# A sign-flipped sine plane, full-row narrow matmuls, merged LayerNorm statistics, other banks, a moved radix-4 inverse and a DMA transpose in a fused S4 convolution and gated MLP

## Chip, cores, metric

One core of one Trainium2 chip. The metric is device microseconds (us) of one execution. Medians are over the fast runs of a kernel; the runs of one kernel here lie within about 1.2% of each other. A profile shows one execution; its span is about 1.8 us shorter than that execution's own time, which need not be the median: the profile of e7 below is of its slowest run, that of e8 of its fastest.

## The reference, cut to what matters

```python
def reference(u, A..., w_gate, w_up, w_down):          # u: 1 x 2048 x 640, bf16
    K = einsum("dn,dnl,dn->dl", C, exp(dt*A*l), dt*B).real   # 640 filters of 2048 taps, 128 modes each
    y = irfft(rfft(pad(layernorm(u))) * rfft(pad(K)))[:L] + layernorm(u) * Dskip
    h = u + y                                            # stage A: the long convolution
    g, v = layernorm(h) @ w_gate, layernorm(h) @ w_up    # stage B: 640 -> 1728
    return h + (sigmoid(g) * v) @ w_down                 # 1728 -> 640
```

Of the kernel before, what the change touches and what calls it, by code (L numbers as in the profile page):

```python
# [26 lines left out]
R4 = (2,)  # L27
AT = {"eb": -38.3, "ea0": -22.2, "tb0": -12.8, "cb": -5.3, "bb0": 10.0, "st0": -13.2, "ta0": 20.7, "ch0": -25.4, "A0": 1.0, "st1": -127.2,
      "st2": -38.2, "st3": 34.0, "tb1": 45.8, "bb1": 28.9, "n0": -8.7, "ta1": 48.0, "ch1": 54.1, "A1": -23.3, "tb2": 49.0, "bb2": 68.1,
      "ea1": 70.7, "n1": 53.4, "ta2": 71.2, "ch2": 33.5, "A2": 32.8, "tb3": 73.0, "bb3": 75.3, "n2": -7.5, "s0": 66.5, "l0": -14.7,  # L30
      "i0": 94.9, "ta3": -15.7, "ch3": -6.7, "A3": -12.7, "n3": 0.8, "s1": 76.0, "l1": -16.4, "i1": 219.0, "i2": -7.7, "LATER": 49.5,
      "LATER2": 98.7, "EARLY": -11.7, "s2": 58.8, "p0": -14.4, "p1": -3.4, "p2": -13.4, "PW": 1, "w0": 29.5, "w1": -19.5, "w2": 66.8,
      "w3": 82.8, "DT": (0, 0, 0, 0), "NG": (1, 0, 0, 0), "TAIL": -45.1, "NA": (1, 2, 0, 0), "SA": (2, 0, 0, 3),
      "K": (42.3, 65.1, 109.8, 202.7), "F": (-18.0, 64.3, 14.3, 46.5), "G": (2.6, 0.5, 2.3, 0)}
# [9 lines left out]
M_SHIFT = (0, 1, 2, 8, 9, 10)  # L44
B_STEPS = ((1, 2, (0, 1, 1), 2), (2, 4, (0, 2, 1), 1), (4, 8, (0, 4, 1), 0), (8, 12, (0, 4, 1), 3), (12, 16, None, 4),
           (16, 18, (0, 16, 8), 5), (18, 21, (12, 17, 2), 5))

# [6 lines left out]
def host_consts():  # L54
    k = np.arange(P)
    fs = np.stack([256 * np.arange(2)[:, None] + k, 511 - 256 * np.arange(2)[:, None] - k], axis=1)
    om = 2 * np.pi * (fs + 0.5) / 1024
    conj = np.array([1.0, -1.0])[:, None]

    G = np.zeros((P, 2, 2, 2, 4, P))  # L60
    n = 4 * np.arange(P)[:, None] + np.arange(4)
    ang = om[None, :, :, None, :] * n[:, None, None, :, None]
    G[:, :, :, 0] = np.cos(ang)
    G[:, :, :, 1] = -np.sin(ang) * conj[None, None, :, :, None]

    lag = np.arange(2048)
    tap = lag.astype(np.float32).astype(ml_dtypes.bfloat16).astype(np.int64)
    KM = np.zeros((P, 2, 2, 2, NK, P))
    for d in range(NB):
        S = np.zeros((2049, 2, 2, P), np.complex128)  # L70
        ls = lag[max(0, LB * d - LB + 1):LB * d + LB]
        np.add.at(S, tap[ls], np.exp(-1j * om[None] * (ls[:, None, None, None] - LB * d)))
        for q, j in enumerate(KD[d]):
            for m in range(4):
                blk = S[B_VAL[4 * j + m] + 8 * np.array(A_EXP)]
                KM[32 * m:32 * m + 32, :, :, 0, KI[d] + q] = blk.real
                KM[32 * m:32 * m + 32, :, :, 1, KI[d] + q] = blk.imag * conj

    IV = np.zeros((P, 4, 2, 2, P))
    nn = 4 * np.arange(P)[None, :] + np.arange(4)[:, None]  # L80
    a = om[:, 0].T[:, None, :, None] * nn[None, :, None, :]
    IV[:, :, :, 0] = np.cos(a) / LB
    IV[:, :, :, 1] = -np.sin(a) / LB
    IV = np.concatenate([IV.reshape(P, 16, P), -IV[:, 1::2].reshape(P, 8, P)], axis=1)

    sel = np.zeros((P, 2, 32))
    sel[32, 0, 31] = 1.0
    for (b, t), rows in SEL.items():
        if b:
            sel[list(rows), 1, FIRST[b] + t - ROWS[b][0]] = 1.0  # L90

    pick = np.zeros((P, 4, 32))
    for c in range(4):
        pick[4 * np.arange(32) + c, c, np.arange(32)] = 1.0
    last = np.zeros((P, 3, 4, NL))
    for c in range(4):
        last[c, 0, c, 0:4] = 1.0
        last[c, 1, c, 4:10] = 1.0
        last[c, 2, c, 10:14] = 1.0
    one = np.zeros((P, 32))  # L100
    one[64, 0] = 1.0
    mult = [4.0 * (31 - 2 * k) for k in range(16)] + [1.0, 2.0]
    dg = np.eye(P)[:, None] * (np.array(mult) * 2.0 ** -13)[None, :, None]
    return {"dg": dg.reshape(P, -1), "ident": np.eye(P), "G": G.reshape(P, -1), "KM": KM.reshape(P, -1), "IV": IV[:, :20].reshape(P, -1), "IVN": IV[:, 20:].reshape(P, -1), "sel": sel.reshape(P, -1),
            "pick": pick.reshape(P, -1), "last": last.reshape(P, -1), "one": one}
# [27 lines left out]
def full_kernel(tc, ins, out):  # L133
# [56 lines left out]
    pick = cload(cp, "pick", [P, 4, 32])  # L190
    last = cload(cp, "last", [P, 3, 4, NL])
# [3 lines left out]
    cor = cp.tile([P, 40], F32, name="cor")  # L195
    xc = cp.tile([P, 40], BF16, name="xc")
    edge = cp.tile([96, D], BF16, name="edge")
    sy.dma_start(edge[64:65, :], ins["A_Dskip"].rearrange("(o d) -> o d", o=1))
# [32 lines left out]
    mg = tabp.tile([P, 2, P], F16, name="mg")  # L231
    ones = tabp.tile([P, 1], F16, name="ones")
    nc.gpsimd.memset(ones[:], 1.0)
    nc.gpsimd.memset(mg[:, 0], MAGIC16 / P)
    nc.gpsimd.memset(mg[:, 1], 0.25 / P)

    def turns(items, o, w):
# [3 lines left out]
        for a in range(2):  # L241
            MM(ps[:, a, 0:m * w], lhsT=mg[:, 0], rhs=bc(ones[:], [P, m * w]), start=True, stop=False)
            for q in range(m):
                src, dk, oo = items[a * m + q]
                for i in range(2):
                    MM(ps[:, a, q * w:q * w + w], lhsT=dg[:, dk, :], rhs=fr[:, src, i, o + oo:o + oo + w], start=False, stop=(q == m - 1 and i == 1))  # L246
        v = ps[:, :, 0:m * w].bitcast(I16).rearrange("p a (n t) -> p a n t", t=2)[:, :, :, 0]

        def quarter():
            for a in range(2):  # L250
                MM(ps[:, a, 0:m * w], lhsT=mg[:, 1], rhs=bc(ones[:], [P, m * w]), start=False, stop=True, skip_group_check=True)
# [8 lines left out]
    st = cp.tile([P, 16, 2, 6], F32, name="ln_st", tag="ln_st")  # L260
# [33 lines left out]
    def trig_b(c):  # L294
        M = T["MB", c] = tabp.tile([P, 2, 6, W], BF16, name="tabMB", bufs=2)
        v, quarter = turns([(0, 16, 0), (0, 17, 0), (0, 15, 0), (1, 16, 0), (1, 17, 0), (1, 15, 0)], W * c, W)
        act_fn(TWO(M[:, 1]), v, AF.Sin, scale=SIN_SCALE16)
        quarter()
        act_fn(TWO(M[:, 0]), v, AF.Sin, scale=SIN_SCALE16)

    def bases_b(c):
        M = T["MB", c]
        for ri in range(2):
            V(M[:, ri], EB[:, :, W * c:W * c + W], M[:, ri], ALU.mult)

# [68 lines left out]
    def chain_b(c):  # L374
        X, M = T["B", c], T["MB", c]
        tS = tabp.tile([P, 8 * W], BF16, name="tS")
        for d0, d1, src, mi in B_STEPS:
# [3 lines left out]
            if src is None:  # L381
                for ri in range(2):
                    s4 = X[:, ri, 0:16, :].rearrange("p (a b) w -> p a b w", a=2)[:, :, 0:2, :]
                    t4, d4 = (v.rearrange("p (a b) w -> p a b w", a=2) for v in (t[:, ri], dst[:, ri]))
                    for o4, pl in ((t4, 1), (d4, 0)):
                        V(o4, s4, bc(M[:, pl:pl + 1, mi:mi + 1, :], [P, 2, 2, W]), ALU.mult)
            else:
                s = X[:, :, slice(*src), :]
                V(t, s, bc(M[:, 1:2, mi:mi + 1, :], [P, 2, n, W]), ALU.mult)
                V(dst, s, bc(M[:, 0:1, mi:mi + 1, :], [P, 2, n, W]), ALU.mult)  # L390
# [6 lines left out]
    def ln_stats(st, mv, src, r):  # L397
        for hh in range(2):
            nc.vector.bn_stats(st[:, r, hh, :], src(r)[:, 320 * hh:320 * hh + 320])  # L399
        nc.vector.bn_aggr(mv[:, r, :], st[:, r, :, :].rearrange("p a b -> p (a b)"))  # L400
# [53 lines left out]
    def kmm(c):  # L454
# [16 lines left out]
        def diagonal(g1, kts):  # L471
# [8 lines left out]
            MM(pv[0:32, 0], lhsT=one[64:65, :], rhs=edge[64:65, dc].rearrange("p (g c) -> p g c", c=4), start=False, stop=True, tile_position=(64, 0))  # L480
            for c4 in range(4):
                MM(pl[:, :, c4], lhsT=last[:, 2, c4, :], rhs=kts[:, :, 80 + c4], start=not c4, stop=False)
            nc.scalar.copy(kv[:, :, 4 * g1:4 * g1 + 4 * GC], ps[:, 0, 0:20 * GC].rearrange("p (j x) -> p j x", j=5))
            for q in range(2):
                MM(ps[0:NL, 1, 0:4 * GC], lhsT=last[0:1, q, 0, :], rhs=kv[0:1, 3 + q, 4 * g1:4 * g1 + 4 * GC], start=False, stop=(q == 1))
# [32 lines left out]
    def prod(c, fs):  # L518
# [7 lines left out]
        for ft in fs:  # L526
            V(t1[:, ft], Z0[:, ft, :, :, o:o + W], S01[:, 0, ft, :, :, o:o + W], ALU.mult)
            V(t2[:, ft], Z0[:, ft, :, :, o:o + W], S01[:, 0, ft, :, ::-1, o:o + W], ALU.mult)
# [10 lines left out]
    def inv0(c, fs=((0, 1),), done=None):  # L539
# [6 lines left out]
        for a in range(2):  # L546
            with tc.issue_after(T["mm"]):
                MM(pv[:, a], lhsT=ident[:], rhs=hv[:, a], start=True, stop=False)
            if a:
                MM(ps[96:128, a, W:2 * W], lhsT=sel[32:33, 0, :], rhs=edge[32:33, o:o + W], start=False, stop=False, tile_position=(32, 96))  # L550
# [102 lines left out]
    st2 = cp.tile([P, 4, 4, 6], F32, name="ln2_st", tag="ln_st")  # L653
# [47 lines left out]
    for r in range(4):  # L701
        for q in range(NC - 2):
            nc.vector.bn_stats(st2[:, r, q, :], h[:, r, W * q:W * q + W])
# [9 lines left out]
    for r in range(4):  # L713
        nc.vector.bn_stats(st2[:, r, NC - 2, :], h[:, r, W * (NC - 2):W * (NC - 1)])

    def done(pv):
        for r in range(4):
            nc.vector.bn_stats(st2[:, r, NC - 1, :], pv[:, r // 2, r % 2])
# [8 lines left out]
    def edges(psp):  # L727
# [6 lines left out]
        sy.dma_start(dcor[:], ct[0:8, :])  # L734
        for b, (t0, t1) in ROWS.items():
            sy.dma_start(xc[16 * FIRST[b]:16 * (FIRST[b] + t1 - t0), :], lanes(x2d[512 * b + 508 + t0:512 * b + 508 + t1, :]))
        sy.dma_start(cor[:], lanes(dcor[:]))
        V(xc[:], xc[:], cor[:], ALU.add)
        sy.dma_start(lanes(dxc[:]), xc[:])
# [88 lines left out]
def mlp(tc, sc, xp, yp, cp, hs, st, mv, rstd, nmr, gu, Wd, ident, oh, ln_coef, ln_stats_act, later, edges, products, inverse, load_h, patch):  # L828
# [23 lines left out]
    def turn(b):  # L852
# [6 lines left out]
        if b and AT["PW"]:  # L859
# [7 lines left out]
        for dc in range(5):  # L867
            pt = psg_p.tile([P, 4, 128], BF16, name="ml_pt", tag="ml_pg")
# [16 lines left out]
    pso.append(pso_p)  # L885
# [5 lines left out]
    for b in range(NB):  # L891
# [29 lines left out]
        for lp in (0, 2):  # L921
            if lp and AT["PW"]:
# [22 lines left out]
            for k in range(2):  # L945
# [3 lines left out]
                for c in range(2):  # L949
                    if b < NB - 1:  # L950
                        tb = Wd[:, 15, 320 * c:320 * c + 320]
# [69 lines left out]
```

## The kernel before: the parts the change touches

The kernel builds tables of complex powers, makes the filter taps from them on TensorE, transforms taps and rows into a block spectrum by matmuls with constant matrices, multiplies the spectra on VectorE, and transforms back. Row block 0 (512 of the 2048 rows) is finished first. Then four MLP blocks run, and the spectral products and inverse transforms of the next row block are woven into each of them. All instructions are traced in one order and then reordered by a scheduler that obeys a table of tuned priorities, `AT`; each engine executes its own list in that order.

```python
R4 = (2,)                       # row block whose inverse uses the radix-4 shortcut (half the matmuls)
AT = {...tuned priorities..., "PW": 1, "DT": (0, 0, 0, 0), "NA": (1, 2, 0, 0), "SA": (2, 0, 0, 3), ...}
# PW: which PSUM banks; DT: DMA transpose per row block; NA / SA: rows normalized / measured by ScalarE

def chain_b(c):                 # powers from powers: complex products, plane 0 cosine, plane 1 sine
    for d0, d1, src, mi in B_STEPS:
        ...
        V(t,   s, sine of step mi,   ALU.mult)
        V(dst, s, cosine of step mi, ALU.mult)
        V(dst[:, 0], dst[:, 0], t[:, 1], ALU.subtract)
        V(dst[:, 1], dst[:, 1], t[:, 0], ALU.add)

def diagonal(g1, kts):          # taps from diagonals, on TensorE, 32-column tiles
    ... 16 matmuls of pick ...
    MM(pv[0:32, 0], lhsT=one[64:65, :], rhs=edge[64:65, dc]..., tile_position=(64, 0))     # one row
    ...
    for q in range(2):
        MM(ps[0:NL, 1, ...], lhsT=last[0:1, q, 0, :], rhs=kv[0:1, 3 + q, ...], ...)        # one row

def turn(b):                    # normalized rows of the next MLP block, transposed for TensorE
    if AT["DT"][b]:
        for i in range(4):
            nc.sync.dma_start(lnT[:, :, i, :], ln2[:, i, :], transpose=True)
        return
    if b and AT["PW"]:          # into the banks of the output accumulators
        ...
    for dc in range(5):         # into the gate banks, one bank per channel chunk
        ...

# one pair of output rows at the end of an MLP block
tb = Wd[:, 15, 320 * c:320 * c + 320]           # staging row for the eviction
nc.scalar.copy(tb, po[k][c][:, 0:320])
nc.vector.tensor_tensor(h2[:, c], tb, h2[:, c], ALU.add)
```

## Time and profile before

| | before |
|---|---|
| median of 3 runs | 361.38 us (360.59 to 361.48) |
| span of the profiled run | 358.8 us |
| busy, share of span | TensorE 91%, VectorE 80%, ScalarE 68% |
| first gate matmul of the MLP | 152.5 us |
| MLP blocks 1 to 4 | 53.8, 54.4, 50.0, 48.1 us |

The cut is by stage: "first gate matmul" is where the convolution of row block 0 ends and the MLP begins; from there the time from one block's first gate matmul to the next is a block's length. The lines themselves are in the prediction.

### The profile page before, as it was taken

How to read it: one execution, taken by the hardware profiler on the slowest of the kernel's cores; microseconds unless marked ns; L12 is line 12 of the kernel's file. 1: busy time of each engine (PE TensorE's matmuls, PEld its weight loads, DVE VectorE, ACT ScalarE, POOL GpSimd, SP SyncE). 2: the span in 40 equal slices, each digit the busy share in tenths (PEclk: the TensorE clock that was granted, in tenths of full speed). 3: DMA queues.
4: the chain of work that ended last, by engine and by line, in shares of the span. 5: the costliest groups of instructions: out<-in, count | busy, mean ns of one | idle time of the engine just before them, and what ended most of it. 6: DMA issues, size and time to landing. Idle time of an engine off the chain costs nothing.

```text
span 358.8 us, 6679 instructions
## 1 busy us (share of the span) xinstructions
PE 324.9 (91%) x2604; PEld 205.7 (57%) x2604; DVE 285.4 (80%) x597; ACT 245.0 (68%) x449; POOL 11.6 (3%) x19
## 2 busy tenths in 40 slices
PE   1598979899999999899999899998699999999995
PEld 1385646777586769744456544455444556644463
DVE  4899999999999979789998999998999931221221
ACT  6999997999899645662767755656655578655500
POOL 1011102000000000100001000001000001000000
PEclk9999999999999999999999999999899999999999
DMA  6990000257007159799400250000030000100011
GB/s 178 337 379 3 16 2 2 83 158 266 13 3 221 75 183 357 177 291 299 184 4 0 74 186 36 2 0 2 1 146 3 0 0 2 55 20 1 0 37 38
DMA packets 29703, 34.37 MB, mean 96 GB/s; under 512 B 16988, under 2 KB 25053, under 8 KB 29416
## 3 DMA queue, kind: packets, MB, share of 16 engines
q1 hardware_dynamic: 29672, 33.95, 29.1%
q8 instruction: 20, 0.33, 0.4%
q14 instruction: 11, 0.09, 0.1%
HBM read 24.72 MB, written 9.21 MB: 95 GB/s over the span
## 4 chain that ended last, share of the span: by engine, by line
PE 41%; DVE 32%; ACT 13%; DMA 7%; issue 3%; SPq 2%; POOL 1%; POOLq 0%; DVEq 0%; ACTq 0%
PE ml_pg L898 8%; PE ml_pu L898 8%; PE ml_po L931 6%; DVE u L684 4%; DVE u L685 4%; PE ps_z L449 3%; PE ps_y L556 3%; PE ps_xk L510 3%; DVE u L687 2%; DVE u L688 2%; PE ps_kv L479 2%; PE pk L468 2%; DVE ln_st L399 2%; ACT zs L450 2%; DMA raw<-in_A_C_re_dram 2%
## 5 line engine op out<-in xcount | busy, mean ns | idle before, releaser
L898 PE MATMUL ml_pg<-lnT,Wg 128*128 128x512 bf16 x260 | 64.8, 379 | 0.7 <-ACT ml_sg L906 0.7
L898 PE MATMUL ml_pu<-lnT,Wu 128*128 128x512 bf16 x260 | 64.9, 379 | 0.5 <-ACT Wd L952 0.4
L931 PE MATMUL ml_po<-Wd,ml_hm 128*128 128x320 bf16 x416 | 59.1, 301 | 0.0
L931 PEld LDWEIGHTS <-ml_hm 128*128 128x128 bf16 x416 | 40.1, 98 | 18.7 <-issue 2.4
L906 ACT ACTIVATE ml_sg<-ml_pg 128x512 bf16<-128x512 f32 x52 | 31.2, 599 | 26.0 <-PE ml_pg L898 14.6
L909 DVE TENSOR_TENSOR ml_hm<-ml_ub,ml_sg 128x512 bf16<-128x512 bf16 x52 | 21.8, 419 | 28.4 <-ACT ml_ub L908 28.4
L908 ACT CAST ml_ub<-ml_pu 128x512 bf16<-128x512 f32 x52 | 30.4, 585 | 20.4 <-PE ml_pu L898 20.2
L898 PEld LDWEIGHTS <-Wu 128*128 128x128 bf16 x260 | 25.4, 98 | 31.5 <-issue 1.0
L898 PEld LDWEIGHTS <-Wg 128*128 128x128 bf16 x260 | 25.4, 98 | 29.2 <-issue 0.9
L449 PE MATMUL ps_z<-u,c_G 128*128 128x320 bf16 x192 | 28.8, 298 | 2.2 <-ACT a_cs L273 0.7
L510 PE MATMUL ps_xk<-kv,c_KM 128*128 128x160 bf16 x320 | 26.6, 232 | 2.4 <-ACT zs L450 1.0
L684 DVE TENSOR_TENSOR u<-Z,S 128x1280 bf16<-128x1280 bf16 x34 | 27.7, 817 | 0.1
L685 DVE TENSOR_TENSOR u<-Z,S 128x1280 bf16<-128x1280 bf16 x34 | 27.7, 816 | 0.0
L246 PE MATMUL ps_t<-fr,c_dg 128*128 128x160 f16 (+1 forms) x180 | 20.0, 240 | 6.1 <-DMA c_dg<-s4c_dg 4.3
L510 PEld LDWEIGHTS <-c_KM 128*128 128x128 bf16 x320 | 23.1, 98 | 4.1 <-issue 3.2
L449 PEld LDWEIGHTS <-c_G 128*128 128x128 bf16 x192 | 18.4, 97 | 10.9 <-issue 3.9
L246 PEld LDWEIGHTS <-c_dg 128*128 128x128 f16 x180 | 14.8, 100 | 13.0 <-issue 4.9
L688 DVE TENSOR_TENSOR u<-u,u 128x1280 bf16<-128x1280 bf16 x23 | 18.8, 817 | 0.0
L687 DVE TENSOR_TENSOR u<-u,u 128x1280 bf16<-128x1280 bf16 x23 | 18.8, 816 | 0.0
L468 PE MATMUL pk<-tabB,tabA 128*128 128x84 bf16 x320 | 16.6, 200 | 2.3 <-ACT kts L469 2.0
L468 PEld LDWEIGHTS <-tabA 128*128 128x128 bf16 x320 | 14.4, 97 | 5.2 <-issue 4.3
L469 ACT CAST kts<-pk 128x420 bf16<-128x420 f32 x32 | 15.6, 543 | 2.5 <-PE pk L468 2.4
(157 smaller groups left out, 549.6 us busy)
## 6 DMA issues: line engine op xcount, KB each, us to landing
dz<-zs SPq DMA_DIRECT2D x12, 320.0 KB, 2.2
c_KM<-s4c_KM SPq DMA_DIRECT2D x1, 2560.0 KB, 12.8
dxk<-xk SPq DMA_DIRECT2D x16, 160.0 KB, 2.4
h<-in_A_u_dram SPq DMA_DIRECT2D x4, 640.0 KB, 3.9
eo<-dz SPq DMA_DIRECT2D x4, 640.0 KB, 4.6
S<-dxk SPq DMA_DIRECT2D x4, 640.0 KB, 7.4
Wg<-in_B_w_gate_dram SPq DMA_DIRECT2D x4, 520.0 KB, 7.9
Wu<-in_B_w_up_dram SPq DMA_DIRECT2D x4, 520.0 KB, 7.7
```

Of the source, the lines that this page charges most:

```text
L246: MM(ps[:, a, q * w:q * w + w], lhsT=dg[:, dk, :], rhs=fr[:, src, i, o + oo:o + oo + w], start=False, stop=(q == m - 1 and i == 1))
L449: MM(ps[:, ri, 0:UH], lhsT=G[:, ft, 0 if b in EO else hf, ri, r, :], rhs=us[b][:, r, o:o + UH], start=(r == rr[0]), stop=(r == rr[-1]))
L468: MM(pk[:, i, :], lhsT=A[:, ri, g].rearrange("p e c -> p (e c)"), rhs=B[:, ri, :, 4 * g:4 * g + 4], start=(ri == 0), stop=(ri == 1))
L510: mm = MM(ps[:, hf, ri * W:ri * W + W], lhsT=KM[:, ft, hf, ri, KI[d] + q, :], rhs=kv[:, j, :], start=(q == 0), stop=(q == len(KD[d]) - 1)).ins
L684: V(t1, z, k[:, :, :, hs_], ALU.mult)
L685: V(t2, z, k[:, :, ::-1, hs_], ALU.mult)
L687: V(s1, s1, t1, ALU.add)
L688: V(s2, s2, t2, ALU.add)
L898: nc.tensor.matmul(ps[:], lhsT=W[:, dc, f0:f0 + 128], rhs=lnT[:, dc].rearrange("p a b -> p (a b)"), start=(dc == 0), stop=(dc == 4))
L906: nc.scalar.activation(sg[:], pg[:], AF.Sigmoid)
L908: nc.scalar.copy(ub[:], pu[:])
L931: nc.tensor.matmul(po[k][c][:, 0:320], lhsT=hm[:, ft, 128 * lr:128 * lr + 128], rhs=Wd[:, ft, 320 * c:320 * c + 320], start=(start and ft ...
```

## The change

The intent is fewer and wider VectorE operations in the convolution, fewer changes of TensorE's tiling mode, and shorter transitions between MLP blocks. The core of the diff:

```diff
-R4 = (2,)
+R4 = (3,)
-AT = {... "PW": 1, "DT": (0, 0, 0, 0), "NA": (1, 2, 0, 0), "SA": (2, 0, 0, 3) ...}
+AT = {... "PW": 0, "DT": (0, 0, 0, 1), "NA": (3, 0, 2, 3), "SA": (1, 0, 0, 3) ...}   # nearly all priorities too
     def bases_b(c):
-        for ri in range(2):
-            V(M[:, ri], EB[...], M[:, ri], ALU.mult)
+        V(m, bc(EB[...], [P, 2, 6, W]), m, ALU.mult)
+        nc.scalar.mul(M[:, 0:3], M[:, 6:9], -1.0)          # the negated sine plane
     def chain_b(c):
+                V(dst, s, cosine, ALU.mult)
+                if mi > 2:
+                    V(t, s[:, ::-1], bc(pair, ...), ALU.mult)   # pair = (-sine, sine)
+                    V(dst, dst, t, ALU.add)
+                    continue
     def diagonal(g1, kts):
-            MM(pv[0:32, 0], lhsT=one[64:65, :], rhs=edge[64:65, dc]..., tile_position=(64, 0))
+            MM(pv[0:32, 0], lhsT=one[0:96, :], rhs=edge[:, dc]..., tile_position=(0, 0))
-                MM(ps[0:NL, 1, ...], lhsT=last[0:1, q, 0, :], rhs=kv[0:1, 3 + q, ...])
+                MM(ps[0:NL, 1, ...], lhsT=last[:, 4 + q, :], rhs=kv[:, 3 + q, ...])
     def prod(c, fs):
-        for ft in fs:  V(t1[:, ft], ...); V(t2[:, ft], ...)
+        V(g(t1[:, f]), z, k, ALU.mult); V(g(t2[:, f]), z, k[:, :, ::-1], ALU.mult)
-        for q in range(NC - 2):
-            nc.vector.bn_stats(st2[:, r, q, :], h[:, r, W * q:W * q + W])
+        nc.vector.bn_stats(st2[:, r, 0, :], h[:, r, 0:2 * W])
+            if lp and AT["PW"] == 2:                        # the three-way split; not run at "PW": 0
...
-                        tb = Wd[:, 15, 320 * c:320 * c + 320]
+                        tb = Wd[:, 14 + k, 320 * c:320 * c + 320]
```

Cut: the fourth matmul made full-row, zeroing of its operand, smaller constants, and buffers that share space.

## The prediction

> **What bounds the kernel now.** I read the page first, then busy time by stage, then the timelines of the stretches where an engine is full, and last the waits at the borders of the stages. The page shows no single owner of the span:
>
> ```profile
> PE 324.9 (91%) x2604; PEld 205.7 (57%) x2604; DVE 285.4 (80%) x597; ACT 245.0 (68%) x449; POOL 11.6 (3%) x19
> ...
> DVE  4899999999999979789998999998999931221221
> ACT  6999997999899645662767755656655578655500
> ```
>
> VectorE is full from about 16 us to 285 us and nearly idle after that, so the last fifth belongs to TensorE alone. Cutting the span at the starts of the four MLP row blocks (152.5, 206.3, 260.7 and 310.7 us, where the gate matmuls begin in the timeline) gives, with columns PE, PEld, DVE, ACT, POOL, clock, DMA share, GB/s:
>
> ```profile
> 0.00:16.50 16.50, 4.83 (x26) 3.13 (x27) 9.49 (x17) 12.94 (x30) 0.97 (x10) 1.00 0.82 241
> 16.50:126.00 109.50, 99.92 (x1113) 75.63 (x1112) 107.67 (x237) 100.39 (x178) 6.11 (x5) 1.00 0.30 106
> 126.00:152.50 26.50, 24.64 (x334) 20.55 (x334) 21.70 (x58) 14.47 (x26) 1.01 (x1) 1.00 0.83 243
> 152.50:206.30 53.80, 51.24 (x309) 28.20 (x307) 51.58 (x100) 34.33 (x65) 1.01 (x1) 1.00 0.45 142
> 206.30:260.70 54.40, 50.03 (x285) 27.04 (x284) 53.37 (x104) 32.83 (x62) 1.45 (x1) 0.97 0.11 37
> 260.70:310.70 50.00, 49.83 (x301) 27.79 (x299) 31.01 (x63) 33.31 (x62) 1.01 (x1) 1.00 0.08 27
> 310.70:358.80 48.10, 44.41 (x249) 23.33 (x246) 10.59 (x25) 16.73 (x29) 0.00 (x0) 1.00 0.08 28
> ```
>
> So: from 16.5 to 126 us (the convolution's tables and spectra) VectorE is 98% busy, with ScalarE at 92% and TensorE at 91% beside it; VectorE binds, but only just. The first two MLP blocks are TensorE work with VectorE full of the later blocks' spectral products; the last two are TensorE work with next to no gap. An MLP block's own work: five up matmuls take 1.08 us in the timeline, 27 such groups 29.2; 104 down matmuls at 3.53 us per 26, 14.1; the 64-row matmuls 1.2; together 44.5. The next block's inverse transform adds 4.35 (32 matmuls at 0.136) or half of that where the radix-4 shortcut is used, as now in the second MLP block. The third block then needs about 50.2 with its transposes and takes 50.0: no slack. The second needs 48 and takes 54.4: some 6 us of waits. The timeline shows most of them at its end:
>
> ```profile
> 251.22 0.40 PE L863 MATMUL ml_pt<-c_ident,ln 128*128 128x128 bf16 x4 [0.35 <-ACT ln L848]
> 254.28 1.87 PE L863 MATMUL ml_pt<-c_ident,ln 128*128 128x128 bf16 x16 [2.66 <-ACT Wd L952]
> ```
>
> The transposes into the output banks wait for an eviction that ScalarE does only after normalizing four rows. After that gap the clock falls (0.83 of full speed on the page's slice), so the next 26 down matmuls took 4.13 us instead of 3.7.
>
> The price of VectorE instructions I take from start to start, not from their recorded length, since records overlap:
>
> ```profile
> 102.62 0.82 DVE L389 TENSOR_TENSOR tS<-tabB,tabMB 128x1280 bf16<-128x1280 bf16 x1
> 103.36 1.55 DVE L390 TENSOR_TENSOR tabB<-tabB,tabMB 128x1280 bf16<-128x1280 bf16 x2
> 104.83 0.48 DVE L391 TENSOR_TENSOR tabB<-tabB,tS 128x640 bf16<-128x640 bf16 x1
> 105.24 0.48 DVE L392 TENSOR_TENSOR tabB<-tabB,tS 128x640 bf16<-128x640 bf16 x1
> 105.64 0.48 DVE L527 TENSOR_TENSOR t<-Z,S 128x640 bf16<-128x640 bf16 x1
> ```
>
> 1280 elements cost 0.74 us and 640 cost 0.40: 0.52 ns an element and only about 0.07 us for an instruction as such. Judged by the recorded 0.82 and 0.48 the fixed part would look twice as large.
>
> **What the Trainium skill says.** "VectorE: DVE Perf Modes", The DRAIN you can't avoid, advises fewer operations rather than fewer semaphores; the 0.07 us above is what one is worth here. "TensorEngine Tiling (Array Packing)", Key Properties: changing the tiling mode drains TensorE. The trace agrees in kind: a pair of one-row matmuls (57.74 to 57.91 us) costs 0.17 us and 0.09 of gap ahead, where full-row matmuls of similar size in the same place come every 0.06. "DMA: Bandwidth & Descriptors", Latency and other measured facts, gives 261 GB/s for a DMA transpose with a broken-up middle dimension. No transpose by DMA is in this trace; its plain 160 KB transfers land 1.8 to 3.2 us after issue.
>
> **The change, part by part.**
> *Complex products.* A sign-flipped sine plane lets a step be two multiplies and one add, all of full width, for two multiplies, a subtract and an add. Element counts are equal, one instruction goes. Four steps in each of four chunks: 16 x 0.07 = 1.1 us less VectorE. The base scaling goes from eight instructions to four (0.3), the products of three chunks from twelve to six (0.4). The price: four ScalarE negations of 480 elements, about 0.5 each by its 0.37 (320 elements) and 0.65 (640): 2.0 us more ScalarE.
> *Statistics.* Eight 160-wide operations at 0.235 become four 320-wide ones at 0.375: 0.4 less. One row of statistics moves from ScalarE to VectorE (two 0.375 and one 0.11: 0.9 more there, 1.6 less on ScalarE). Five more rows are normalized on ScalarE: 1.8 off VectorE (0.36 each), 4.1 on ScalarE (0.82 each).
> Sum for the convolution: VectorE 1.1 + 0.3 + 0.4 + 0.4 - 0.9 + 1.8 = 3.1 us less; ScalarE 2.0 - 1.6 + 4.1 = 4.5 more. In the stage at 16.5 to 126 us this puts both near 105 us of 109.5: the two meet.
> *Full-row narrow matmuls.* 8 + 16 + 4 one-row matmuls lose their change of mode; 0.07 to 0.1 each is some 2 us of TensorE, of which I count 0.7, since TensorE is the waiting party in most of that stage.
> *Radix-4 moved from the second to the third transformed block.* 16 matmuls (2.2 us) go from the third MLP block to the second, and eight VectorE operations (4.1 us) the other way. The sum is zero; only the waits in the second block can give something: 0.4.
> *Banks.* The words promise a three-way split, but the new constant is 0, so that branch is not run. What runs is the one-bank-per-chunk path: transposes go to the gate banks, the second pair of output accumulators returns to the output banks. Transposes no longer wait for the late eviction (1.79 and 2.66 us), but each now needs all four normalized rows, and five copies at 0.5 apart pace them: in the first block from 200.6 to 203.1 against 202.4 now, in the second about level. I count 0.5 of loss. A second staging row for the evictions removes the one 0.39 us wait seen at 207.9.
> *DMA transpose for the last block.* 20 matmuls and a 0.17 wait go (305.25 to 306.80: 1.55 us of a stage with no slack). The rows are normalized one by one until 305.1; the result is needed at 310.7 - 1.5 = 309.2. The last 160 KB has 4.1 us for it; issue to landing of about 2.5 (plain transfers here) fits. Gain 1.5.
> Sum: 3.0 + 0.7 + 0.4 - 0.5 + 0.4 + 1.5 = 5.5 us. The reordered priorities I cannot cost; I give them nothing. 361.4 - 5.5 = 355.9.
>
> **Rivals.**
> *ScalarE becomes the bound of the convolution.* For it: 100.4 + 4.5 of 109.5 us, with every chunk's chain now passing through a ScalarE negation. Against: it idles about 12 us from 126 to 152.5, and the first two steps of a chain need no negated plane. The 3.0 would become 0 or -2: 359 to 361.
> *The DMA transpose is slow.* Four in a row at some 4 us each would land near 319, with TensorE idle for 8 us and a cold clock after: 363 to 366. For it: nothing here shows its time. Against: only the last of three possible blocks was switched, the one with quiet queues (27 GB/s).
> *The new order pays.* The many changed priorities fit a search rather than a hand edit, and about 12 us of the first 152.5 are idle on VectorE around the borders (7 in the first 16.5, 5 from 126). Recovering a third of it on top: 351 to 353.
>
> **Range and chances.** 355.9 is 1.5% below; 2% lies at 354.2, a little under it. The resource terms carry perhaps 2 us of error, the order and the DMA 3 us each, mostly independent: 4 to 5 us in all. So 349.5 to 361.5 eight times in ten; faster by over 2% 0.36, within 2% 0.58, slower 0.06, the last being the slow transpose together with a worse order.
>
> **What would show it.** Right: the first gate matmul about 3.5 us earlier (near 149), VectorE busy near 282, ScalarE near 250, the third MLP block near 46.5 us, the second no shorter than 54, and no PE gap at the last block's start. Wrong: a first gate matmul earlier by over 6 us (the order, not the operations, was the lever); ScalarE gaps gone and VectorE waiting for negated planes; or TensorE waiting for a DMA into the transposed rows.

## The result

| | before | after |
|---|---|---|
| median | 361.31 us (360.59 to 361.48, 4 runs) | 357.56 us (357.33 to 358.02, 4 runs) |
| ratio of fast runs | | 0.9902, 95% interval 0.9885 to 0.9919 |
| profiled span, clock | 358.8 us, 0.995 | 355.8 us, 0.994 |
| first gate matmul | 152.5 us | 153.4 us |
| MLP blocks 1 to 4 | 53.8, 54.4, 50.0, 48.1 us | 53.5, 54.1, 46.8, 48.0 us |

A ratio is the mean time of one kernel's fast runs over that of the other's of the same rounds, so it is not quite the ratio of the medians quoted. The change gains 1.0%: within 2%, and within the predicted range. The stage table shows at once that the parts did not come where the prediction put them. The page after:

```profile
PE 321.6 (90%) x2584; PEld 205.2 (58%) x2584; DVE 283.0 (80%) x566; ACT 245.8 (69%) x455; POOL 11.4 (3%) x20
...
DVE  3799999999998889869999899999899951211222
ACT  6999999999999763672766845547845678455500
```

VectorE lost 31 instructions and 2.4 us. ScalarE gained only 0.8 us, not 4.5: by the stages it gained 3.6 before the MLP and lost 3.5 in the third block. The prediction forgot that the DMA transpose also takes the block's evictions of transposes from ScalarE (five of 0.59 us; e5 below has 17 of them, this kernel 12). By stage, with the columns PE, PEld, DVE, ACT, POOL, clock, DMA share and GB/s:

```profile
0.00:16.50 16.50, 5.25 (x29) 3.80 (x30) 8.59 (x14) 12.52 (x28) 1.32 (x11) 1.00 0.80 224
16.50:126.00 109.50, 98.08 (x1090) 75.15 (x1090) 104.97 (x211) 104.07 (x184) 6.03 (x5) 0.98 0.31 108
126.00:153.40 27.40, 24.52 (x354) 21.35 (x354) 24.85 (x57) 14.80 (x28) 1.01 (x1) 1.00 0.88 254
153.40:206.90 53.50, 51.61 (x309) 28.32 (x307) 49.78 (x97) 34.71 (x67) 1.01 (x1) 1.00 0.43 132
206.90:261.00 54.10, 51.07 (x301) 28.17 (x299) 53.11 (x101) 33.23 (x64) 1.01 (x1) 1.00 0.11 39
261.00:307.80 46.80, 46.71 (x266) 25.12 (x264) 31.15 (x67) 29.79 (x59) 1.01 (x1) 1.00 0.15 43
307.80:355.80 48.00, 44.38 (x249) 23.32 (x246) 10.58 (x25) 16.73 (x29) 0.00 (x0) 0.99 0.08 28
```

In the second row VectorE fell from 107.67 to 104.97 and ScalarE rose from 100.39 to 104.07, as predicted, yet the MLP starts 0.9 us *later*. From 16.5 us to the first gate matmul TensorE was busy 124.56 us of 136.0 before and 122.60 of 136.9 after: it has 2.0 us less to do and idles 2.9 us more. One slice shows where, before and then after:

```profile
75.00:90.00 15.00, 14.77 (x191) 11.29 (x190) 14.93 (x35) 14.40 (x31) 0.00 (x0) 1.00 0.56 195
```

```profile
75.00:90.00 15.00, 11.99 (x154) 9.33 (x152) 14.86 (x32) 14.52 (x28) 0.00 (x0) 1.00 0.62 206
```

TensorE missed 2.8 us here, and did that work later: in its instruction list 56 matmuls of the far spectra stand behind the first transpose for the MLP, against 34 before. At some 0.07 us each (start to start) that is 1.5 us between the transposes and the gate. A rival is the clock: TensorE's granted clock is 0.50 from 34.2 to 37.6 us after and 1.00 there before. But e5 and e7 below have 1.00 there too, with the same convolution code, and their gates (153.1 and 153.8 us) lie on both sides of 153.4.

The gain is all in the third MLP block, 50.0 to 46.8 us. Its transposes are now DMA transposes and its inverse has half the matmuls. The timeline of its end (SPq is the DMA queue's issuing engine):

```profile
300.80 5.27 SPq L867 DMA_TRANSPOSE lnT<-ln  x4
...
304.25 3.70 PE L946 MATMUL ml_po<-Wd,ml_hm 128*128 128x320 bf16 x26
...
307.79 1.24 PE L909 MATMUL ml_pg<-lnT,Wg 128*128 128x512 bf16 x5
```

The down matmuls run into the next block's gate matmuls without a gap. The queue was busy issuing each transpose of 160 KB for a median of 1.27 us, and each landed 2.6 us after issue, so the last one (issued at 304.8) was there at 307.4, only 0.4 us before it was needed.

The second block took over 16 matmuls (2.2 us) and still came out at 54.1: its waits shrank from 4.4 us in all to 3.0 (length less TensorE's busy time), and its clock rose from 0.97 to 1.00. The waits at its end were 0.35 and 2.66 us before, followed by 4.13 us instead of 3.7 for 26 slower matmuls. After:

```profile
250.74 3.69 PE L946 MATMUL ml_po<-Wd,ml_hm 128*128 128x320 bf16 x26 [0.87 <-ACT Wd L967]
254.26 0.50 PE L881 MATMUL ml_pt<-c_ident,ln 128*128 128x128 bf16 x3
255.35 0.45 PE L881 MATMUL ml_pt<-c_ident,ln 128*128 128x128 bf16 x5 [0.58 <-ACT ln L858]
```

The bracket gives TensorE's idle time and who ended it. The end of the block now holds these two waits and one of 0.17 us; another 1.25 and 0.15 us, for a gate product of VectorE, stand at 245.3 us, just before the lines shown.

### The profile page after: what moved, and what is told of

Its sections match the earlier page's. It is cut to its first block, busy times and chain, and to the rows that moved or that the text cites. A ratio compares the mean times of both kernels' runs of the same rounds, so it can differ in the third digit from the quotient of the medians.

```text
span 355.8 us, 6614 instructions
## 1 busy us (share of the span) xinstructions
PE 321.6 (90%) x2584; PEld 205.2 (58%) x2584; DVE 283.0 (80%) x566; ACT 245.8 (69%) x455; POOL 11.4 (3%) x20
## 4 chain that ended last, share of the span: by engine, by line
DVE 24%; PE 16%; issue 15%; DMA 4%; SPq 3%; ACT 1%; POOL 1%; POOLq 0%; DVEq 0%; ACTq 0%
PE ml_po L946 5%; DVE u L693 5%; DVE u L694 5%; PE ml_pg L909 5%; PE ml_pu L909 4%; DVE u L696 3%; DVE u L697 3%; DVE ml_hm L920 2%; DMA dcor<-corr 2%; DVE VR L704 2%; SPq L821 2%; DMA Wl<-in_B_w_up_dram 1%; SPq L822 1%; DVE Z L673 1%; DVE y L701 1%
## 5 line engine op out<-in xcount | busy, mean ns | idle before, releaser
L457 PE MATMUL ps_z<-u,c_G 128*128 128x320 bf16 x192 | 30.6, 309 | 3.9 <-ACT zs L458 1.7
```

The costliest lines, as they stand in the source:

```text
L457: MM(ps[:, ri, 0:UH], lhsT=G[:, ft, 0 if b in EO else hf, ri, r, :], rhs=us[b][:, r, o:o + UH], start=(r == rr[0]), stop=(r == rr[-1]))
```

## The experiments

Each run was timed over several rounds beside the kernel before (e1 to e4 on one chip, e5 to e8 on one, e9 to e12 on one; medians of before 361.11, 360.88 and 360.93 us). e10 computes something else on purpose. Times are medians; "gate" is the first gate matmul in the profile.

Three things limit what small differences mean. The changed kernel was timed apart from them, beside a median of before of 361.31 us, so differences of a few tenths between medians of different chips are not read. A gate from one profile is uncertain too: e5 to e8 and e12 change nothing in the convolution, and up to the gate their profiles have the changed kernel's instructions in the same order on TensorE, VectorE and ScalarE, yet their gates lie between 152.7 and 153.9 us. Part of the spread of equal runs goes with the granted clock: of the 33 timings of the kernel before in these rounds, the five at clock 1.00 took 359.2 to 360.0 us and the six at 0.989 or 0.990 took 360.6 to 362.5.

| run | median us | ratio to before (95%) | gate | MLP blocks |
|---|---|---|---|---|
| after | 357.56 | 0.9902 (0.9885 to 0.9919) | 153.4 | 53.5, 54.1, 46.8, 48.0 |
| e1 | 358.12 | 0.9922 (0.9898 to 0.9947) | 152.3 | 53.9, 54.9, 46.9, 48.0 |
| e2 | 367.45 | 1.0186 (1.0160 to 1.0212) | 162.8 | 53.9, 54.2, 46.8, 48.0 |
| e3 | 363.53 | 1.0078 (1.0053 to 1.0103) | 160.7 | 53.5, 54.1, 46.8, 48.0 |
| e4 | 358.69 | 0.9949 (0.9922 to 0.9975) | 154.5 | 53.5, 54.1, 46.8, 48.0 |
| e5 | 358.81 | 0.9956 (0.9928 to 0.9984) | 153.1 | 53.5, 54.1, 48.0, 48.2 |
| e6 | 360.00 | 0.9984 (0.9956 to 1.0011) | 153.9 | 53.5, 52.1, 50.7, 48.0 |
| e7 | 358.04 | 0.9932 (0.9904 to 0.9959) | 153.8 | 54.9, 54.1, 46.7, 47.8 |
| e8 | 357.72 | 0.9929 (0.9891 to 0.9966) | 152.7 | 53.5, 54.1, 46.7, 48.0 |
| e9 | 357.74 | 0.9913 (0.9892 to 0.9933) | 153.6 | 53.5, 54.1, 46.8, 48.0 |
| e10 | 357.20 | 0.9887 (0.9866 to 0.9908) | 153.1 | 53.5, 54.1, 46.8, 48.0 |
| e11 | 358.83 | 0.9938 (0.9920 to 0.9956) | 154.6 | 53.5, 54.1, 46.8, 48.0 |
| e12 | 362.07 | 1.0029 (1.0009 to 1.0050) | 153.1 | 51.3, 57.8, 49.5, 48.0 |

### e1: the old convolution with the new MLP

```diff
 # kernel before
-R4 = (2,)   "PW": 1   "DT": (0, 0, 0, 0)   tb = Wd[:, 15, ...]
+R4 = (3,)   "PW": 0   "DT": (0, 0, 0, 1)   tb = Wd[:, 14 + k, ...]
```

> The kernel before with only the MLP part of the change: radix-4 moved to the last block, transposes of the last block by DMA, the one-bank-per-chunk transposes, the second staging row. Theory (all of the gain is made in the MLP and the convolution gives nothing): the first gate matmul stays near 152.5 us, the third MLP block takes about 46.8 us, the whole about 357.4 or a little less (361.3 - 3.9). Rival (the convolution's part is needed for the gain, or the MLP part wins only because VectorE had less to do before): 359.5 to 361.5.

Measured: 358.12 us, 0.6 above the changed kernel (the intervals of the two ratios overlap), with the changed kernel's third and fourth block to 0.1. So the MLP's settings carry nearly the whole gain, and the rewritten convolution next to none.

### e2: the new operations under the old order and assignment of rows

```diff
 # kernel after: the whole AT of the kernel before, except
+"PW": 0, "DT": (0, 0, 0, 1)
```

> The changed kernel with all its new operations and its MLP settings, but with the priorities, the row split between the engines and so the order of the convolution of before. Theory (the new operations do save VectorE time in the convolution, and the new order with its rows on ScalarE spends it): first gate matmul at 149.5 to 151, whole 354 to 355.5. Rival 1 (VectorE was not the bound; operations saved there are worth nothing in any order): first gate near 152.5, whole near 357.4. Rival 2 (the new operations themselves cost, by the negation's place in the chain): first gate after 153, whole 358 or more.

Measured: 367.45 us, outside all that was expected but "358 or more", and the first gate matmul 9.4 us later than in the changed kernel. TensorE once waits 9.7 us for one row that VectorE normalizes, and its clock falls. The slice (same columns as before):

```profile
30.00:45.00 15.00, 3.92 (x16) 2.05 (x17) 14.48 (x26) 7.81 (x13) 0.49 (x1) 0.56 0.04 10
```

Priorities tuned for one set of operations were wrong for the other. The operations therefore cannot be judged with the scheduler free to reorder; this made e9 to e11 necessary.

### e3: the normalized rows back to their engines of before

```diff
-"NA": (3, 0, 2, 3), "SA": (1, 0, 0, 3)
+"NA": (1, 2, 0, 0), "SA": (2, 0, 0, 3)
```

> The changed kernel with only the split of statistics and normalized rows set back (one row of statistics to ScalarE, five normalized rows back to VectorE: ScalarE about 2.5 us less, VectorE about 1 more). Theory (ScalarE binds the new convolution): first gate at 151.5 to 152.5, whole 355.5 to 356.5. Rival (VectorE still binds, or the order does): first gate at 153.5 to 154.5, whole 357.5 to 358.5.

Measured: 363.53 us, outside both expectations; the gate is 7.4 us later in the profile, which is of the slowest run (364.94 us). That is far more than the VectorE work that came back (1.8 us of rows, less 0.9 of statistics): again the order no longer fits. This run shows that assignment and order belong together; it does not price the assignment.

### e4: the negation on VectorE

```diff
-        nc.scalar.mul(M[:, 0:3], M[:, 6:9], -1.0)
+        nc.vector.tensor_scalar(M[:, 0:3], M[:, 6:9], -1.0, None, ALU.mult)
```

> The changed kernel with only the four negations of the sine planes moved from ScalarE (about 0.5 us each) to VectorE (about 0.2 us each). ScalarE-bound theory: first gate 1 to 2 us earlier, whole about 356. Rival (VectorE-bound): 0.8 us later, whole about 358.4. Rival (neither, the tail after 126 us binds): no change within 0.3 us.

Measured: 358.69 us, the gate 1.1 us later. Relieving ScalarE did not help; by the numbers the rival fits, that VectorE binds (0.8 us later, 358.4). But the scheduler also reordered other instructions on TensorE, VectorE and ScalarE, so neither reading is settled here; e9 and e10 hold the order.

### e5: no DMA transpose

```diff
-"DT": (0, 0, 0, 1)
+"DT": (0, 0, 0, 0)
```

> The changed kernel with the last block's transposes back on TensorE. My prediction's step (1.5 us): third MLP block 46.8 -> about 48.4 us, whole about 359.1. Rival (the DMA transposes hide nothing that mattered, since the rows arrive late either way): no change. The other blocks stay at 53.5, 54.1 and 48.0.

Measured: third block 48.0 instead of 46.8, median 1.25 us up. The DMA transpose is worth 1.2 us in its block; 1.5 was predicted.

### e6: radix-4 back in the second block's inverse

```diff
-R4 = (3,)
+R4 = (2,)
```

> The changed kernel with the radix-4 shortcut back in the block transformed during the second MLP block. Theory A (moving it is zero-sum, as predicted, and the second block gained by the banks): second block 54.1 -> 51.9, third 46.8 -> 49.0, whole unchanged at 357.6. Theory B (the second block is bound by VectorE or by the chain into the next block, so matmuls put there are free): second block stays at 54, third 49.0, whole 359.8.

Measured: second block 2.0 us shorter, third 3.9 us longer, so the placement is worth 1.9 us in the MLP. Matmuls explain 2.2 of the third block's 3.9. Most of the rest is one wait:

```profile
285.01 1.24 PE L909 MATMUL ml_pg<-lnT,Wg 128*128 128x512 bf16 x5 [1.60 <-ACT ml_sg L917]
```

ScalarE had itself waited 2.38 us for a gate product that VectorE ran behind the last spectral products, which now end at about 285 us. My reading, not tested apart, is that they start relatively later in the third block because the second is shorter: VectorE's debt moves from block to block. This returns in e12.

### e7: the old banks

```diff
-"PW": 0
+"PW": 1
```

> The changed kernel with the banks of before for the transposes and the second pair of output accumulators. Theory A (the banks took 2 to 3 us of waits out of the second block's end): second block 54.1 -> 56.5, first 53.5 -> 53.8, whole about 360.3. Theory B (my prediction: banks are a loss of 0.5 on balance): second block 54.1 or less, whole 357.0 to 357.6.

Measured: in the profile only the first block changes, 1.4 us longer; the median rises by 0.5, within the intervals, and the profile is of the slowest of the six runs (359.14 us). In the trace, the end of the first block:

```profile
202.27 1.85 PE L873 MATMUL ml_pt<-c_ident,ln 128*128 128x128 bf16 x16 [2.38 <-ACT Wd L967]
...
204.70 4.20 PE L946 MATMUL ml_po<-Wd,ml_hm 128*128 128x320 bf16 x26
```

The transposes wait 2.38 us for an output bank, and the next 26 matmuls take 4.20 us rather than 3.7: the granted clock is 0.50 from 202.3 to 205.7 us. The Trainium skill ("TensorE: Matmul & The Clock Gate", What's actually happening) puts the fall of the clock after an idle window of about 3.4 us, the window running free; here a gap of 2.38 us was enough. The kernel before has the same banks and waits 1.79 us at this place at clock 1.00, and its first block is 53.8 us, only 0.3 above the changed kernel's. So most of the 1.4 us is the slow clock, which the wait of before did not bring at this place. The second block keeps its 54.1 us even with the old wait (2.35 us) and clock 0.97.

### e8: the three-way split that the new code offers

```diff
-"PW": 0
+"PW": 2
```

> The changed kernel with the three-way split of banks that its words name but its constant leaves off: transposes go to the up banks, the second pair of accumulators to one gate pair and one output tile. If the 0.84 and 0.87 us that the down matmuls wait for an eviction at the middle of the first two blocks are real cost: blocks of 52.7 and 53.3, whole about 356. Rival (the wait only moves to the transposes behind, which need the normalized rows): within 0.3 of 357.6.

Measured: all block lengths as after, median 357.72. The 0.84 and 0.87 us waits for an accumulator disappear (the 52 matmuls of two pairs run as one group), and the same time reappears in front of the transposes, which wait for the rows:

```profile
191.30 7.24 PE L946 MATMUL ml_po<-Wd,ml_hm 128*128 128x320 bf16 x52
...
199.70 0.23 PE L881 MATMUL ml_pt<-c_ident,ln 128*128 128x128 bf16 x1 [0.58 <-ACT ln L858]
```

So the end of the first two blocks is, as I read it, set by the chain from the last inverse row over its statistics to the last normalized row, not by banks. Down start to last normalized row takes 13.1 us in the first and 14.8 in the second block after; TensorE has 11.2 us of down matmuls to cover it. In the third block, where VectorE is free, it is 10.9 us and nothing waits.

### e9: more VectorE operations, every engine's order fixed

```diff
 # kernel after, plus issue-order edges (no waits) that hold all four engines to the changed kernel's order
-                    V(dst, dst, t, ALU.add)
+                    V(dst[:, 0], dst[:, 0], t[:, 0], ALU.add)
+                    V(dst[:, 1], dst[:, 1], t[:, 1], ALU.add)
 # and likewise the base scaling and the products in two halves: 26 operations more
```

> The changed kernel with 26 of VectorE's merged operations split in two again (the base scaling, the third operation of each chain step, the products), as the kernel before has them, and every engine's instruction order held to that of the changed kernel by issue-order edges, so that only the cost of VectorE changes: 26 x 0.07 = 1.8 us more. If VectorE binds the convolution, as the prediction had it, the first gate matmul comes 1.8 us later (155.2) and the whole is 1.8 us slower than the changed kernel (about 359.3). If the three engines hold each other up in a fixed order (the theory after the result), only a part arrives: 0.3 to 1.0 us. If nothing of VectorE's matters, under 0.3.

The instruction lists, apart from the 26 extra halves, are the same on every engine. Measured: 357.74 us, 0.2 above the changed kernel; the gate 0.2 us later. The sums of the view by stretches up to 152 us, first the changed kernel's and then this one's:

```profile
sum 152.00, PE 126.61 PEld 99.19 DVE 137.01 ACT 130.46 POOL 8.36; mean PE 42.20 PEld 33.06 DVE 45.67 ACT 43.49 POOL 2.79
```

```profile
sum 152.00, PE 125.83 PEld 98.71 DVE 138.30 ACT 130.22 POOL 7.93; mean PE 41.94 PEld 32.90 DVE 46.10 ACT 43.41 POOL 2.64
```

VectorE did work 1.3 us longer (0.05 us an operation), and about 0.2 of it arrived. One place where it was absorbed, in the changed kernel and then here:

```profile
116.63 0.83 DVE L335 TENSOR_TENSOR tabA<-tabEA,tabE 128x1280 bf16<-128x1280 bf16 x1 [2.09 <-PE pk L476]
```

```profile
116.87 0.82 DVE L336 TENSOR_TENSOR tabA<-tabEA,tabE 128x1280 bf16<-128x1280 bf16 x1 [1.73 <-PE pk L478]
```

VectorE waits for TensorE at this point, and its wait shrank by 0.36 us. The 0.2 itself is smaller than the scatter of the gate, and the two ratios alone (0.9913 and 0.9902) would not exclude that all 1.3 arrived; gate, median and the absorbed wait together speak for a small part. So VectorE, 96% busy from 16.5 to 126 us, most likely does not bind this stage as a whole.

### e10: no negation, order fixed

```diff
-        nc.scalar.mul(M[:, 0:3], M[:, 6:9], -1.0)
+        nc.scalar.mul(M[:, 0:3, 0:2], M[:, 6:9, 0:2], -1.0)
-                    pair = M[:, mi - 3:mi + 4:6, :]
+                    pair = M[:, mi:mi + 4:3, :]          # wrong planes, on purpose
```

> The changed kernel with the negation cut from 480 elements to 6 and the step reading planes that exist anyway (wrong results on purpose), the order held as in the run before: ScalarE is relieved of four times 0.4 us and VectorE of waiting for the plane. If ScalarE is the bound of the convolution (the first rival), the first gate matmul comes 1.5 us earlier (151.9) and the time is about 356.0. If VectorE binds and the plane is never waited for, nothing changes (within 0.3). If the engines hold each other up, 0.3 to 0.8 us earlier.

Measured: 357.20 us, the gate 0.3 us earlier. The same view:

```profile
sum 152.00, PE 125.17 PEld 98.18 DVE 137.27 ACT 129.12 POOL 8.36; mean PE 41.72 PEld 32.73 DVE 45.76 ACT 43.04 POOL 2.79
```

ScalarE was relieved of 1.3 us and about 0.3 arrived, again no more than the gate's scatter; the 1.5 us expected of a ScalarE bound did not. So ScalarE most likely does not bind the stage as a whole either, and the first rival falls with the same reserve. (The comparison with the reference passed even so: these terms are too small for its tolerance. The kernel is not a valid version.)

### e11: one-row narrow matmuls again, order unchanged

```diff
-            MM(pv[0:32, 0], lhsT=one[0:96, :], rhs=edge[:, dc]..., tile_position=(0, 0))
+            MM(pv[0:32, 0], lhsT=one[64:65, :], rhs=edge[64:65, dc]..., tile_position=(64, 0))
 # likewise the two of last and the one of sel: 28 matmuls in all
```

> The changed kernel with the narrow matmuls on one row again, as before the change; the order of every engine comes out the same. The prediction counted 0.7 us for the full rows, of at most 2: then the time is about 358.3. If TensorE is only the waiting party there, under 0.3; if every change of mode arrives, 2 us (359.6).

The lists came out the same without edges. Measured: 358.83 us, 1.3 us more; the gate 1.3 us later. What the eight matmuls of the first kind waited for:

```profile
L488 PE MATMUL ps_kv<-edge,c_one x8: 204/205/205, 54.3 to 135.3; 1*32 1x80 bf16 x8
...
  issue: 3.0, 8
```

In the changed kernel the same view lists no such wait, and the matmuls follow each other closely:

```profile
129.42 0.22 PE L488 MATMUL ps_kv<-edge,c_one 96*32 96x80 bf16 x1
129.48 0.32 PE L490 MATMUL ps_kv<-kts,c_last 128*14 128x20 bf16 x4
```

The full-row form is 15 ns longer itself (219 to 221 against 204) and removes the idle time ahead. Ahead of the other 20 matmuls the idle time is the same in both (0.8 us for `last`, 0.8 for `sel`): what was gained lies at these eight. Of the three things priced in a fixed order, this is the only one on TensorE and the only one whose effect is clear of noise (ratio 0.9938 against 0.9902).

### e12: a version meant to beat both

```diff
-"DT": (0, 0, 0, 1)
+"DT": (0, 1, 1, 1)
 # and the four small statistics operations of row blocks 1 to 3 on GpSimd in place of VectorE
```

> A version meant to beat both: the changed kernel with the DMA transpose for all three later blocks, and the four small statistics operations of these blocks on GpSimd in place of VectorE, where they queue behind products of 0.74 us. If the ends of the first two MLP blocks hang on the chain from the last inverse row to the last normalized row and the transfers stay quiet, each of these blocks becomes 1.5 to 2.8 us shorter (about 51 and 52) and the time is 352 to 355. The rival: the transposes queue behind 640 KB loads, or land later than TensorE can wait for, and the clock falls: blocks of 53.5 or more, and the time as it was or worse.

Measured: 362.07 us, slower than both. The first block became 2.2 us shorter as hoped (51.3). The transposes landed in 2.6 us here too and TensorE never waited for them. But the second block is 3.7 and the third 2.7 us longer. The second block's main waits:

```profile
216.59 1.24 PE L909 MATMUL ml_pg<-lnT,Wg 128*128 128x512 bf16 x4 [0.81 <-ACT ml_sg L917]
...
244.54 0.45 PE L946 MATMUL ml_po<-Wd,ml_hm 128*128 128x320 bf16 x2 [1.45 <-DVE ml_hm L920]
246.94 0.31 PE L957 MATMUL ml_po<-Wd,ml_hm 64*128 64x320 bf16 x1 [1.95 <-DVE ml_hm L931]
```

Neither expectation fits: the transposes were fast, but the time they freed was lost again. TensorE now waits for VectorE's gate products, which stand behind spectral products; that the shorter first block left these undone is my reading. In numbers, 57.8 - 54.1 = 3.7: the waits are 6.3 us (57.83 less 51.52 busy) against 3.0, which is 3.3 more; busy time is 0.4 more although 1.5 us of transposes are gone, so the matmuls themselves ran some 1.9 us longer at the lower mean clock (0.97 against 1.00). VectorE's work over the three blocks is the same (133.0 against 134.0 us). GpSimd did not shorten the end of the chain: from the last square to the first normalized row took 3.0 us in the second block, against 1.9 us in the changed kernel. The two edits were not run apart and the scheduler reordered the MLP for them, so their shares are open; so is whether new priorities would save the idea.

## Why the prediction was right, and where its steps were not

The number was right (355.9 predicted, 357.56 measured), and so were range and class; the sum behind it was not. A gain of 3.7 us that did not come in the convolution and 2.1 us more than predicted in the MLP partly cancelled. That the number held is luck.

- **"VectorE binds, but only just" in the convolution: most likely wrong.** This was the largest term, -3.0. The work went as computed: 2.7 us less VectorE in the stage. But e9 puts 26 operations back at fixed order and about 0.2 us arrive. Being 96 to 98% busy was read as being the bound. Three engines at 90% or more hand work round in fixed lists, and the busiest of them need not be on the path. What does set the pace of this stage is not shown.
- **The rival "ScalarE becomes the bound": most likely wrong too.** e10 takes 1.3 us from ScalarE and gains about 0.3.
- **Full-row narrow matmuls, -0.7: mechanism right, size too small.** 1.3 us (e11). Of "some 2 us" only a third was counted because "TensorE is the waiting party"; most of it did arrive. The idle time saved lies at eight of the 28 matmuls, where the prediction priced every one; the pair at 57.74 us from which it read the price is among the other 20.
- **"The reordered priorities I cannot cost; I give them nothing."** This step probably hid the largest effect. At the new order, held fixed, the merged operations (0.2) and the full rows (1.3), less the negation (0.3), are worth about 1.2 us, so the gate should have come near 151.3; it came at 153.4. By this difference some 2 us, uncertain by about 1 by the scatter of gates, lie in the new order together with the new assignment of rows and the parts of the change not priced (the wider statistics, the smaller constants); no run isolates them. e2 and e3 show that the two cannot be separated by undoing one: 7 to 9 us are lost then. In which instructions they arise is open beyond the slice shown above and the 22 far-spectrum matmuls that moved behind the first transpose. The gate of one and the same convolution order already lies between 152.7 and 153.9 in e5 to e8, so 1 us of it is no more than such scatter.
- **DMA transpose, -1.5:** 1.2 (e5). Right. The slow-DMA rival fell: landing 2.6 us, near the 2.5 estimated from plain transfers. (The 1.8 to 3.2 us quoted for these left out other 160 KB loads of the same trace, which landed after up to 7.3 us.)
- **Radix-4, "the sum is zero", -0.4:** 1.9 us (e6). The count was right, "the sum is zero" was not. With the old banks the 16 matmuls cost the second block nothing (54.4 us before, 54.1 in e7); with the new ones they cost it 2.0 us (52.1 in e6, 54.1 after), but then the third block without the shortcut waits 1.60 us for gate products on top of its 2.2 us of matmuls. The prediction had both facts, waits in the second block and no slack in the third, and did not put them together. Of its "some 6 us of waits" only 4.4 were idle time; part of the rest was the slower clock.
- **Banks, +0.5:** the loss did not show, and the sign is probably wrong: 1.4 us gained in the first block of one profile (e7), most of it a spell of slower clock, none in the second; 0.5 us in the median, not clear of noise.
- **Second staging row, -0.4:** not run by itself.

The MLP gave 3.9 us where 1.8 were predicted, and the convolution cost 0.9 where a gain of 3.7 was predicted.

## What to carry to other kernels

Before pricing a saving, ask whether the engine is on the path, not how busy it is: at fixed order, 1.3 us of a 96% busy engine were worth about 0.2, and small gaps closed on TensorE were worth 1.3. When a scheduler reorders, hold the instruction order fixed and change one cost; undoing an edit under tuned priorities measured mostly the priorities here (e2, e3). Before reading tenths of a microsecond from one profile, look at how far runs with the same order scatter. Move work into blocks that already wait, and check where the time freed at one block's end is owed later.

## What the Trainium skill lacked or had wrong

- "VectorE: DVE Perf Modes" (Rules for kernel authors) advises minimizing the operation count. True of VectorE's own time, 0.05 us an operation in e9 (26 operations, 1.3 us), but it does not say that this need not reach the end: about 0.2 us did.
- "TensorEngine Tiling (Array Packing)" (Key Properties) says that a mode switch drains TensorE and gives no figure. e11: with 28 one-row matmuls the time is 1.3 us longer. The idle time ahead of eight of them, 3.0 us in the trace (0.37 each), vanished with the full rows, and ahead of the other 20 it did not change; no more than 1.3 us of it reached the end.
- "TensorE: Matmul & The Clock Gate" (What's actually happening): the clock falls after an idle window of about 3.4 us. In e7 the clock fell to 0.50 after a wait of 2.38 us, for 3.4 us, and 26 matmuls took 4.20 instead of 3.7 us; in e6 it was 0.50 from 245.0 to 248.4 us, after no wait longer than 1.70. A wait of 1.79 us before (first block) left it at 1.00.
- "DMA: Bandwidth & Descriptors" (Latency and other measured facts) gives 261 GB/s for a transpose with a broken-up middle dimension. Here the data of the last 160 KB moved between 306.0 and 306.8 us at 191 GB/s, but issuing one took the queue a median of 1.27 us, so that four in a row moved only 107 GB/s from the first issue to 306.9 us. Issue to landing was 2.6 us.
